# A planned instruction order made anew: planner durations set to measured occupancy, the order kept as a list of ranks

## The chip, the cores and the metric

The kernel runs on one core of a Trainium2 chip. The metric is the device time of one launch in microseconds (us): a median of 256.72 us over three runs before the change (256.70 to 256.86). The profile is that of one execution, with a span of 255.3 us.

## What is computed

Sliding-window attention with sink tokens, followed by a ResMLP block. For each of 4 batches there are 8 heads, 768 positions and head size 64:

```python
scores = scale * np.matmul(q, k.transpose(0, 1, 3, 2))
keep = (pos[None, :] < n_sink) | ((rel >= 0) & (rel < window))      # n_sink 4, window 128
a = softmax(np.where(keep, scores, -1e9))
x = heads_side_by_side(np.matmul(a, v))                              # [4, 768, 512]
a1 = alpha1 * x + beta1
u = x + lam * np.einsum('ts,bsd->btd', w_tok, a1)
a2 = alpha2 * u + beta2
out = u + lam * (np.maximum(a2 @ w_ch1, 0.0) @ w_ch2)                # w_ch1 512 x 2048, w_ch2 2048 x 512
```

Inputs and output are float32; the kernel multiplies in float16.

## The kernel before, in words

A batch is cut into six tiles of 128 tokens. Its work on TensorE falls into these groups:

- `tp`: transposes of q and k into `qkT`, in batches 0 and 1. In batches 2 and 3 DMA transposes do this, issued by SP.
- `S`, `sk`: scores of a key tile against 256 queries, and of the sink keys. ScalarE makes `E` with an exponential; VectorE or GpSimd masks it, except where a bias was added in the scores.
- `pv`: the product with v, whose row sums come with it; VectorE divides (L850, L851) and so makes `x`. GpSimd multiplies by lam times alpha1 (`tm`, L869), and VectorE or GpSimd adds the beta term (`xh`, L872).
- `tok`: the token mix, six matmuls of 512 columns for a tile (L956). VectorE adds it to `x` (L963), and ScalarE or GpSimd casts the sum to `u16` (line L356 or L358, a helper for all copies).
- `uT`: `u` transposed, in two chunks of three tiles each. In batch 0 TensorE transposes (`uTp`, L997); in the others it is a DMA transpose of each tile in SP's queue (L1015). ScalarE (L980) or VectorE (L982) then multiplies by alpha2 and adds beta2, one instruction for each of four column blocks of a chunk.
- `h`: the first MLP product, 16 feature blocks for each chunk, four matmuls of 384 columns each (L1036), and a ReLU on ScalarE or VectorE into `hT` (L1042, L1044). A chunk's `h` can start only when its four `uT` blocks are there.
- `ch` (batch 0, L1221) and `P` (batches 1 to 3, L1153): the second MLP product. In batches 1 to 3 it is one level of Strassen's scheme: seven products `P1` to `P7` of half the size, for which VectorE makes sums of `hT` (L1094 to L1097), and sums of w2 once (`w2s`, L1068).

None of this is executed in the order in which the code names it. Every group, copy and load is a task, given to `Plan.add` with a priority, the engines which could do it with a duration in ns for each, the tasks that it needs, and the buffers that it uses. `Plan.run` is a list scheduler: it repeatedly takes the task that can start first, by its own clock of every engine, with the priority deciding between equals, picks the engine that would finish it first, and adds `SEEN` ns until others see the result. It also models DMA rings (`lands`: packets, ns for each) and the shared port of VectorE and GpSimd. `Plan.emit` then issues the instructions in that order. The durations therefore never reach the chip; they decide only the order in each engine's queue, the engine of tasks with a choice, and which physical buffer each tile gets. In the first 36 us the planner also puts filler matmuls (`idle`, L349) where it expects TensorE to wait.

Before the change the priorities are those written in the code, jittered by 30 seeds one after the other (`TURNS`, through `shuffle`).

Loads on SP's queue are held back by `gates`: three tiny DMAs that read a quarter of w1 each, so that SP stands still until that quarter is there.

The functions which the change touches:

Of the kernel before, what the change touches and what calls it, by code (L numbers as in the profile page):

```python
# [10 lines left out]
FP16 = mybir.dt.float16  # L11
# [6 lines left out]
SEEN = {PE: 200, ACT: 60, DVE: 60, POOL: 70}  # L18
# [93 lines left out]
class Plan:  # L112
# [19 lines left out]
    def run(self, prio):  # L132
# [16 lines left out]
        free = {PE: 0.0, ACT: 3500.0, DVE: 3200.0, POOL: 500.0, SP: 0.0}  # L149
# [18 lines left out]
        def pick():  # L168
            best = None
            spare = {k: sorted(h for h, x in zip(homes[k], busy[k]) if not x) for k in homes}  # L170
            for r, i in open_:
# [12 lines left out]
                for e in t.engs:  # L184
                    at_e = max(free[e], at)
                    if e == POOL or (e == DVE and t.port):
                        at_e = max(at_e, port)
                    key = (at_e + FW * t.engs[e], at_e, r, at_e + t.engs[e], i, e)
                    if own is None or key < own:
                        own = key  # L190
# [55 lines left out]
    def emit(self, turns):  # L246

        prio = [t.prio for t in self.tasks]
        for seed in turns:
            prio = shuffle(prio, seed)  # L250
        for t, e, start, stop, idle in self.run(prio):
# [10 lines left out]


def shuffle(prio, seed):

    rnd = random.Random(seed)
    if seed >= 200000:
        lo = rnd.choice((12.0, 24.0, 40.0, 60.0, 100.0, 130.0, 160.0, 200.0, 230.0, 260.0, 300.0, 330.0))
        hi, wide = lo + 60.0, 10.0 ** rnd.uniform(0.3, 1.3)
    elif seed < 100000:  # L270
        lo, hi, wide = -2200.0, 8.0, 10.0 ** rnd.uniform(0.7, 2.7)
    else:
        lo = rnd.choice((0.0, 0.0, 0.0, 50.0, 100.0, 200.0))
        hi, wide = lo + 60.0, 10.0 ** rnd.uniform(0.3, 1.3)
    share = 10.0 ** rnd.uniform(-2.5, -1.0)
    return [p + rnd.gauss(0.0, wide) if lo <= p < hi and rnd.random() < share else p for p in prio]
# [3 lines left out]
def kernel(  # L280
# [128 lines left out]
    gates = sb.tile([1, 32], FP16, tag="pt_1", bufs=1, name="gates")  # L409
# [7 lines left out]
    TURNS = (13523, 134113, 50022, 128275, 136711, 187603, 125671, 100730, 14946, 163131, 178432, 158827, 183776, 137680, 153375, 26742, 367527, 307353, 376563, 212018, 255075, 397706, 218147, 375675, 393913, 224567, 207692, 352780, 243076, 346008)  # L417
# [74 lines left out]
    def load_qk(p, b, hp, t, wait=None):  # L492
# [8 lines left out]
        if b < XB:  # L501
            src = src.rearrange("h (p r) d -> p h (r d)", p=P)
            done["nat", b, hp, t] = add(
                p, {SP: 480}, lambda e: nc.sync.dma_start(bf.t, src), [wait], [bf], lands=(16, {(0, 0, 1): 85, (0, 1, 0): 140}.get((b, hp, t), 72)))
        else:
            src = src.rearrange("h s d -> (h s) d").rearrange("(x p) d -> p x d", p=P)
            done["nat", b, hp, t] = add(
                p, {SP: 700}, lambda e: nc.sync.dma_start(
                    bf.t.rearrange("p e (r d) -> p (e r) d", r=NR), src), [wait], [bf], lands=(96, 19.0))

    def load_v(p, b, r, wait=None):
        bf = vn[b, r] = Buf("vnat", None, None, f"vnat{b}_{r}")
        done["vn", b, r] = add(
            p, {SP: 550}, lambda e: nc.sync.dma_start(
                bf.t, v[b, :, r * P : (r + 1) * P, :].rearrange("h p d -> p h d")),
            [wait], [bf], lands=(64, 19.0))
# [3 lines left out]
    def load_v0(p, G, r):  # L520
# [4 lines left out]
        else:  # L525
# [7 lines left out]
            uses=[bf], lands=(32, 19.3))  # L533
# [14 lines left out]
    def load_w(p, key, src):  # L548
        bf = wst[key] = Buf("wst", None, None, f"wst_{key}")
        done["wst", key] = add(  # L550
            p, {SP: 400}, lambda e: nc.sync.dma_start(bf.t, src), [done.get(("w1", GATES[0]))], uses=[bf], lands=(16, 90))

    def load_w1(p, i):
# [4 lines left out]
            lands=(32, 96), since=W1_SINCE)  # L558

    def gate(i):  # L560

        add(-3000, {SP: 420}, lambda e: nc.sync.dma_start(
# [14 lines left out]
    ANY = {DVE: 560, ACT: 831, POOL: 829}  # L577
# [6 lines left out]
    def trans(p, b, hp, t, engs, evac, cast_p=None, wait=None):  # L584
# [43 lines left out]
        if b >= XB:  # L628
            done["qkT", b, hp, t] = add(
                p, {SP: 1240}, lambda e: nc.sync.dma_start_transpose(  # L630
                    o.t[:, 2 * hp + t, :].rearrange("p (r i) -> p r i", r=NR),
                    n16().rearrange("p r i -> p (r i)")),
                [a] + prior, [bn, o], lands=(6, 100))
# [5 lines left out]
    def sinks(p, b, Gs=(0, 1)):  # L639
# [24 lines left out]
        a = add(p, {DVE: 400 if n == 1 else 600, ACT: 440}, ksf, qk + [done.get(("sk", b - 1, 0))], [o], port=True)  # L664
        a = add(p + 0.1, {PE: 215}, mm, [a], [o, pt], mode="col")
        done["sk", b, Gs[0]] = a
        done["es", b, Gs[0]] = add(p + 0.2, {ACT: 595}, ex, [a], [pt, es[b]])

    def fill_vs(p, b, G=None):
# [13 lines left out]
        done["vs", b, G] = add(p + 0.1, {DVE: 150 + 68 * n}, ev, [a, done["vs1"]] + prior, [pt])  # L683
# [6 lines left out]
    def scores(p, b, j, Gs, bias=False):  # L690
# [51 lines left out]
        for G, hps, n, pS, eT in units:  # L742
# [7 lines left out]
            x_ = add(p + 0.1, {ACT: 170 + 2 * n * w * 0.835}, ex, [a], [pS, eT])  # L750
            if not bias:
# [11 lines left out]
                c = {DVE: 60 + 2 * n * w * 0.66}  # L763
                if b and j:
                    c[POOL] = 2 * (150 + n * w * 0.9)
# [6 lines left out]
    def scores_by_pair(p, j, bias):  # L772
# [5 lines left out]
        for hp in range(2):  # L778
# [19 lines left out]
            xs.append(add(p - 1000 + 40 * hp + 0.1, {ACT: 170 + 2 * w * 0.835}, ex, [a], [pS, eT]))  # L798
        if not bias:
# [5 lines left out]
            xs = [add(p - 999.8, {DVE: 60 + 4 * w * 0.61}, mk, xs, [eT], port=True)]  # L805
# [3 lines left out]
    def pv(p, b, r, G):  # L809
# [44 lines left out]
        a = done["x", b, r, G] = add(p + 0.1, {DVE: 640}, norm, [a], [po, rec, bx])  # L854
        prior = [done.get(("tok", b - 1, ti)) for ti in range(NR)]
        if b == 0:
            c = slice(256 * G, 256 * G + 256)

            def half(e):
# [4 lines left out]
                p + 0.3, {POOL: 730}, half, [a, done["la1"]], [bx, bh], port=True)  # L864
        elif G == 1:
# [5 lines left out]
            def plus(e):  # L871
                engine[e].tensor_add(bh.t, bt.t, lb1_b)  # L872

            a = add(p + 0.3, {POOL: 1350}, mul, [a, done["x", b, r, 0], done["la1"]], [bx, bt], port=True)
            done["xh", b, r, 1] = add(
                p + 0.4, {POOL: 1390, DVE: 690}, plus, [a, done["lb1b"]] + prior, [bh, bt], port=True)
            done["xb", b, r] = None
        if G == 1 and b == 0:
            def beta(e):
# [5 lines left out]
                (1.5 if r < 3 else 4.5) if b == 0 else p + 0.4, {DVE: 740}, beta,  # L885
# [11 lines left out]
    def cast_v0(p, G, rs):  # L897
# [3 lines left out]
            p, {POOL: 190 + 215 * n, ACT: 195 + 213 * n, DVE: 215 + 115 * n},  # L901
# [7 lines left out]
    def cast_wtok(p, ti):  # L909
# [8 lines left out]
        def cast(e):  # L918
# [8 lines left out]
        a = done["rs", ti] = add(p, {ACT: 850, DVE: 870}, cast, [done["wtn", ti]], [src, w])  # L927
        a = add(p + 0.1, {PE: 330}, tr, [a, done["iden"]], [w, pt])
        done["wtokT", ti] = add(
            p + 0.2, {DVE: 560, ACT: 810}, lambda e: copy(e, wtokT[:, :, ti * P : (ti + 1) * P], pt.t),  # L930
            [a], [pt])

    def cast_w2(p, i):
        for a in range(4 * i, 4 * i + 4):
            src = wst[f"w2_{a - a % 2}"]
            done["w2", a] = add(
                p, {DVE: 980, POOL: 1400},
# [9 lines left out]
    def tok(p, b, ti):  # L947
# [26 lines left out]
        a = done["u", b, ti] = add(p + 0.1, {DVE: 690}, ua, [a, done["xb", b, ti]], [pt, bx])  # L974
        done["u16", b, ti] = add(p + 0.2, {ACT: 620, POOL: 640}, uc, [a], [bx, bu])
# [9 lines left out]
    def uTp(p, b, chk, cp):  # L985
# [15 lines left out]
        for ci in range(2):  # L1001
            c = 2 * cp + ci
            done["uT", b, chk, c] = add(
                p + 0.1 + 0.01 * ci, {DVE: 470, ACT: 670},
# [4 lines left out]
    def uTx(p, b, ti):  # L1009

        if (b, 0) not in uT:
# [3 lines left out]
            p, {SP: 1220}, lambda e: nc.sync.dma_start_transpose(  # L1015
                bo.t[:, :, ti * P : (ti + 1) * P], bu.t),
            [done["u16", b, ti]], [bu, bo], lands=(6, 100))
# [3 lines left out]
        for c in range(NC):  # L1021
            o = (c, slice(chk * NTOK, (chk + 1) * NTOK))
            done["uT", b, chk, c] = add(
                p + 0.1 + 0.01 * c, {DVE: 380, ACT: 700},
# [3 lines left out]
    def mlp1(p, b, chk, fi):  # L1028
# [20 lines left out]
        done["h", b, chk, fi] = add(p + 0.1, {ACT: 493, DVE: 556}, relu, [a], [ph, bh])  # L1049
# [7 lines left out]
    def w2_sums(p):  # L1057

        for g in range(HF // 2):
# [5 lines left out]
            def sub(o, i0, i1, after, n_):  # L1065
# [3 lines left out]
                return add(p + 4 * g + n_, {DVE: 420, POOL: 1400}, f_, after, [bw], port=True)  # L1069
# [47 lines left out]
    def prod(p, b, what, nt):  # L1117
# [46 lines left out]
        def plus(p, bx, cols, more):  # L1164
# [3 lines left out]
            return add(p, {DVE: 400}, f_, [a, u_] + more, [pc, bx])  # L1168

        def store(p, bx, ti, cols, after):  # L1170
            n_ = (cols.stop - cols.start) // 64
            add(p, {SP: 480}, lambda e: nc.sync.dma_start(out[b, ti * P : (ti + 1) * P, cols], row(bx)[:, cols]),
# [3 lines left out]
        if what == "P1":  # L1176
            done["read", b, what, nt] = add(p + 0.1, {ACT: 390, DVE: 350}, lambda e: copy(e, bt.t, pc.t), [a], [pc, bt])
# [4 lines left out]
        elif what == "P6":  # L1182
# [3 lines left out]
            u = add(p + 0.1, {DVE: 400}, u2, [a, done["read", b, "P1", nt]], [pc, bt])  # L1186
# [4 lines left out]
            def ob(e):  # L1191
# [4 lines left out]
            done["U12", b, nt] = add(p + 0.3, {POOL: 760, DVE: 400}, ot, [u, done["u16", b, nt]], [bt, top], port=True)  # L1196
            done["U2", b, nt] = add(
                p + 0.2, {POOL: 1300, DVE: 690}, ob,
# [13 lines left out]
    def mlp2(p, b, ti, part):  # L1212
# [16 lines left out]
        if part == 3:  # L1229
# [4 lines left out]
            a = add(p + 0.1, {DVE: 690}, oa, [a, done["u16", b, ti]], [pc, bx])  # L1234
            add(p + 0.2, {SP: 480}, lambda e: nc.sync.dma_start(
# [194 lines left out]
```

The softmax here doesn't subtract the row's maximum and nothing guards it: scores larger than these inputs give would overflow.

## Time and profile before

| what | value |
|---|---|
| time | 256.72 us |
| span of the profiled execution | 255.3 us |
| TensorE (PE) busy | 247.4 us, 97% |
| VectorE (DVE) busy | 190.0 us, 74% |
| ScalarE (ACT) busy | 142.6 us, 56% |
| GpSimd (POOL) busy | 88.3 us, 35% |
| TensorE clock granted | 0.999 |
| moved by DMA | 38.8 MB, 152 GB/s over the span |

In the page, "busy" is the union of an engine's instructions; the ends of matmuls are modelled, so gaps of TensorE are better taken from starts. `A <- B` in the view of waits reads: A stood idle until B released it. The timeline merges instructions of one form and gives the start, the time from the first start to the last end, and in brackets the idle time of the engine before it with its releaser.

### The profile page before, as it was taken

How to read it: one execution, taken by the hardware profiler on the slowest of the kernel's cores; microseconds unless marked ns; L12 is line 12 of the kernel's file. 1: busy time of each engine (PE TensorE's matmuls, PEld its weight loads, DVE VectorE, ACT ScalarE, POOL GpSimd, SP SyncE). 2: the span in 40 equal slices, each digit the busy share in tenths (PEclk: the TensorE clock that was granted, in tenths of full speed). 3: DMA queues.
4: the chain of work that ended last, by engine and by line, in shares of the span. 5: the costliest groups of instructions: out<-in, count | busy, mean ns of one | idle time of the engine just before them, and what ended most of it. 6: DMA issues, size and time to landing. Idle time of an engine off the chain costs nothing.

```text
span 255.3 us, 5519 instructions
## 1 busy us (share of the span) xinstructions
PE 247.4 (97%) x2174; PEld 160.9 (63%) x2174; DVE 190.0 (74%) x402; ACT 142.6 (56%) x236; POOL 88.3 (35%) x108
## 2 busy tenths in 40 slices
PE   8999998999999999899999999999999999999994
PEld 7754645675555544456678676558668666667883
DVE  6777998696878878578889997877789764136782
ACT  2689845989848035688971225867571125775000
POOL 7409802344445330159653460735310101000000
PEclk9999999999999999999999999999999999999999
DMA  6998999999943998599778689501000156000105
GB/s 202 195 223 292 216 230 392 373 370 218 218 73 115 186 260 190 117 205 220 155 138 182 125 191 251 85 3 21 3 0 3 59 167 146 0 0 3 63 4 185
DMA packets 86130, 38.80 MB, mean 152 GB/s; under 512 B 73540, under 2 KB 80460, under 8 KB 86104
## 3 DMA queue, kind: packets, MB, share of 16 engines
q1 hardware_dynamic: 82320, 35.14, 56.5%
q0 software_dynamic: 3744, 3.28, 8.1%
q8 instruction: 17, 0.28, 0.5%
q14 instruction: 9, 0.07, 0.1%
q10 hardware_dynamic: 40, 0.03, 0.0%
HBM read 29.91 MB, written 6.29 MB: 142 GB/s over the span
## 4 chain that ended last, share of the span: by engine, by line
PE 88%; DMA 4%; DVE 3%; POOL 1%; issue 1%; ACT 1%; POOLq 0%; ACTq 0%
PE h L1036 33%; PE P L1153 21%; PE tok L956 11%; PE ch L1221 8%; PE pv L825 5%; PE S L724 4%; DMA n<-in_q_dram 4%; DVE uT L982 1%; PE S L719 1%; PE tp L614 1%; PE pv L818 1%; POOL n L497 1%; PE wT L916 1%; ACT uT L980 1%; DVE w2f L1068 1%
## 5 line engine op out<-in xcount | busy, mean ns | idle before, releaser
L1036 PE MATMUL h<-uT,w1f 128*128 128x384 f16 x512 | 91.9, 326 | 2.7 <-DVE uT L982 1.3
L1036 PEld LDWEIGHTS <-w1f 128*128 128x128 f16 x512 | 47.3, 98 | 34.5 <-issue 5.5
L1042 ACT ACTIVATE hT<-h 128x384 f16<-128x384 f32 x99 | 48.3, 492 | 26.1 <-PE h L1036 25.6
L1153 PEld LDWEIGHTS <-hT 128*128 128x128 f16 x408 | 39.8, 98 | 6.7
L746 ACT ACTIVATE E<-S 128x1024 f16<-128x1024 f32 (+1 forms) x39 | 37.9, 1001 | 7.5 <-PE S L724 3.7
L869 POOL TENSOR_TENSOR tm<-x,la_b 128x512 f32<-128x512 f32 x18 | 26.2, 1454 | 26.3 <-DVE xh L872 19.1
L956 PE MATMUL tok<-xh,wtokT 128*128 128x512 f16 x144 | 33.4, 379 | 0.0
L356 ACT CAST u<-x 128x512 f16<-128x512 f32 x19 | 11.7, 618 | 31.2 <-DVE x L963 31.1
L1153 PE MATMUL P<-w2f,hT 128*128 128x256 f16 x216 | 25.9, 273 | 0.0
L1166 DVE TENSOR_TENSOR x<-x,P 128x256 f32<-128x256 f32 x45 | 18.3, 418 | 8.2 <-PE P L1153 7.9
L1044 DVE TENSOR_SCALAR hT<-h 128x384 f16<-128x384 f32 x29 | 15.8, 553 | 10.9 <-PE h L1036 10.5
L956 PEld LDWEIGHTS <-wtokT 128*128 128x128 f16 x144 | 14.0, 98 | 14.6
L1221 PE MATMUL ch<-w2f,hT 128*128 128x512 f16 x96 | 23.0, 379 | 0.0
L1153 PE MATMUL P<-w2s,hT 128*128 128x256 f16 x192 | 22.8, 273 | 0.0
L851 DVE TENSOR_TENSOR x<-pv,rec 128x256 f32<-128x256 f32 x48 | 20.4, 424 | 1.7
L358 POOL CAST vfs<-vnat 128x512 f16<-128x512 f32 x18 | 15.0, 840 | 16.2 <-DMA vnat<-in_v_dram 16.0
L963 DVE TENSOR_TENSOR x<-x,tok 128x512 f32<-128x512 f32 x24 | 16.2, 684 | 5.7 <-PE tok L956 5.7
L356 ACT CAST n<-nat 128x768 f16<-128x768 f32 x16 | 13.2, 829 | 10.8 <-DMA nat<-in_q_dram 8.8
L825 PEld LDWEIGHTS <-E 128*128 128x128 f16 x328 | 15.2, 97 | 6.0 <-issue 1.6
L825 PE MATMUL pv<-vfs,E 128*128 128x65 f16 x328 | 17.9, 194 | 0.0
L358 POOL CAST u<-x 128x512 f16<-128x512 f32 x5 | 3.1, 621 | 34.8 <-DVE x L963 21.1
L1221 PEld LDWEIGHTS <-hT 128*128 128x128 f16 x96 | 8.6, 98 | 9.1 <-issue 0.2
(131 smaller groups left out, 327.4 us busy)
## 6 DMA issues: line engine op xcount, KB each, us to landing
out_dram<-x SPq DMA_DIRECT2D x21, 256.0 KB, 2.8
nat<-in_q_dram SPq DMA_DIRECT2D x13, 384.0 KB, 5.3
nat<-in_k_dram SPq DMA_DIRECT2D x13, 384.0 KB, 5.7
vnat<-in_v_dram SPq DMA_DIRECT2D x18, 256.0 KB, 5.2
wst_w<-in_moe_w_ch_dram SPq DMA_DIRECT2D x8, 512.0 KB, 7.4
wtn<-in_moe_w_tok_dram SPq DMA_DIRECT2D x6, 384.0 KB, 4.7
w1f<-in_moe_w_ch_dram POOLq DMA_DIRECT2D x4, 512.0 KB, 11.1
v<-in_v_dram SPq DMA_DIRECT2D x12, 128.0 KB, 6.4
```

The costliest lines, as they stand in the source:

```text
L356: nc.scalar.copy(o, i)
L358: engine[e].tensor_copy(o, i)
L746: nc.scalar.activation(eT.t, pS.t[:, :, 0 : n * w].rearrange("p e (i w) -> p e i w", i=n), AF.Exp, scale=scale)
L825: nc.tensor.matmul(po.t[:, hl, :], eT.t[:, e_, off + i, c : c + P], vf[j][:, h, :], start=(r < 2 and n == 0), stop=(n == len(parts) - 1 an ...
L851: nc.vector.tensor_mul(bx.t[:, 4 * G : 4 * G + 4, :], po.t[:, :, 0:D], rec.t.to_broadcast([P, 4, D]))
L869: engine[e].tensor_mul(bt.t, bx.t.rearrange("p h d -> p (h d)"), la1_b)
L956: nc.tensor.matmul(pt.t, wtokT[:, si, ti * P : (ti + 1) * P], hs[si].t, start=(si == 0), stop=(si == NR - 1))
L1036: nc.tensor.matmul(ph.t, w1f[:, c, fi * P : (fi + 1) * P], bu.t[:, c, chk * NTOK : (chk + 1) * NTOK], start=(c == 0), stop=(c == NC - 1))
L1042: nc.scalar.activation(bh.t[:, fi, :], ph.t, AF.Relu)
L1153: nc.tensor.matmul(pc.t, hh[:, nt * P : (nt + 1) * P], w(fi), start=(first and n_ == 0), stop=(n_ == HF - 1), skip_group_check=True)
L1166: nc.vector.tensor_add(row(bx)[:, cols], row(bx)[:, cols], pc.t)
L1221: nc.tensor.matmul(pc.t, bh.t[:, fi, nt * P : (nt + 1) * P], w2f[:, fi, :], start=(fi == 0), stop=(fi == NF - 1))
```

## The change

It is for a plan whose clock is nearer to that of the chip, and an order searched for on it. Four things change:

1. The durations of nearly all tasks on ScalarE, VectorE, GpSimd and SP are set to the measured occupancy of the engine (how long until it can take the next), which is shorter than the instruction's latency; in exchange `SEEN`, the time until a reader may start, grows from 60 to 150 ns on ScalarE and VectorE. DMA packets get new times too, and GpSimd and SP start later in the plan (500 to 1600 ns, 0 to 800 ns).
2. The order is no longer code priorities jittered by seeds, but a list of 1143 ranks, one for each task (`ORDER`).
3. A string of digits (`PINS`) can fix the engine of a task: 0 leaves the choice, n takes the n-th of its engines.
4. The tile `gates` gets a place of its own instead of sharing one with a later buffer, since two of the gates now stand late in SP's queue.

```diff
-SEEN = {PE: 200, ACT: 60, DVE: 60, POOL: 70}
+SEEN = {PE: 200, ACT: 150, DVE: 150, POOL: 70}
...
-    def run(self, prio):
+    def run(self, prio, pin=None):
...
-        free = {PE: 0.0, ACT: 3500.0, DVE: 3200.0, POOL: 500.0, SP: 0.0}
+        free = {PE: 0.0, ACT: 3500.0, DVE: 3200.0, POOL: 1600.0, SP: 800.0}
...
-                for e in t.engs:
+                one = pin[i] if pin and pin[i] <= len(t.engs) else 0
+                for n, e in enumerate(t.engs):
+                    if one and n + 1 != one:
+                        continue
...
-    def emit(self, turns):
-        prio = [t.prio for t in self.tasks]
-        for seed in turns:
-            prio = shuffle(prio, seed)
-        for t, e, start, stop, idle in self.run(prio):
+    def emit(self, prio, pin):
+        for t, e, start, stop, idle in self.run(prio, pin):
...
-    gates = sb.tile([1, 32], FP16, tag="pt_1", bufs=1, name="gates")
+    gates = const.tile([1, 32], FP16, name="gates")
...
-    TURNS = (13523, 134113, 50022, 128275, 136711, 187603, 125671, 100730, 14946, 163131, 178432, 158827, 183776, 137680, 153375, 26742, 367527, 307353, 376563, 212018, 255075, 397706, 218147, 375675, 393913, 224567, 207692, 352780, 243076, 346008)
+    ORDER = (
+        66, 71, 1075, 86, 311, 53, 58, 60, 63, 54, 64, 61, 65, 67, 81, 95, 68, 69, 72, 62, 77, 74,
...
-                p, {SP: 480}, lambda e: nc.sync.dma_start(bf.t, src), [wait], [bf], lands=(16, {(0, 0, 1): 85, (0, 1, 0): 140}.get((b, hp, t), 72)))
+                p, {SP: 480}, lambda e: nc.sync.dma_start(bf.t, src), [wait], [bf], lands=(16, {(0, 0, 1): 85, (0, 1, 0): 140}.get((b, hp, t), 68)))
...
-        add(-3000, {SP: 420}, lambda e: nc.sync.dma_start(
+        add(-3000, {SP: 790}, lambda e: nc.sync.dma_start(
...
-            x_ = add(p + 0.1, {ACT: 170 + 2 * n * w * 0.835}, ex, [a], [pS, eT])
+            x_ = add(p + 0.1, {ACT: 50 + 2 * n * w * 0.85}, ex, [a], [pS, eT])
...
-                c = {DVE: 60 + 2 * n * w * 0.66}
+                c = {DVE: 70 + 2 * n * w * 0.53}
...
-            a = add(p + 0.3, {POOL: 1350}, mul, [a, done["x", b, r, 0], done["la1"]], [bx, bt], port=True)
+            a = add(p + 0.3, {POOL: 1250}, mul, [a, done["x", b, r, 0], done["la1"]], [bx, bt], port=True)
...
-                p, {DVE: 980, POOL: 1400},
+                p, {DVE: 612, POOL: 1240},
...
-        a = done["u", b, ti] = add(p + 0.1, {DVE: 690}, ua, [a, done["xb", b, ti]], [pt, bx])
-        done["u16", b, ti] = add(p + 0.2, {ACT: 620, POOL: 640}, uc, [a], [bx, bu])
+        a = done["u", b, ti] = add(p + 0.1, {DVE: 610}, ua, [a, done["xb", b, ti]], [pt, bx])
+        done["u16", b, ti] = add(p + 0.2, {ACT: 530, POOL: 575}, uc, [a], [bx, bu])
...
-        done["h", b, chk, fi] = add(p + 0.1, {ACT: 493, DVE: 556}, relu, [a], [ph, bh])
+        done["h", b, chk, fi] = add(p + 0.1, {ACT: 395, DVE: 480}, relu, [a], [ph, bh])
...
-    plan.emit(TURNS)
+    plan.emit(ORDER, [int(c) for c in PINS])
```

The instructions themselves, their number on TensorE (2174 matmuls, 106 of them filler) and the data moved stay as they were. In the new order, the groups of TensorE around the places of which the prediction speaks are these (`b` the batch; a group of `h`, four matmuls; of `tok`, six; of `ch`, four; of `P`, eight):

| place | before | after |
|---|---|---|
| batch 0, `tok` to `h` | six `tok`, `uTp` x2, `h` | five `tok`, `uTp` x2, `tok` of tile 5, `h` |
| batch 1, `tok` to `h` | `tok` 1, 0, 2, `ch`, `tok` 3, 4, 5, `h` | `tok` 0, 2, 1, `ch`, `tok` 5, `ch`, `tok` 3, `ch`, `tok` 4, `h` |
| batch 2, late `tok` to chunk 1 of `h` | `tok` 4, then 2 `h`, 2 `S`, 2 `pv`, 6 `P` | `tok` 3, then 2 `h`, 2 `S`, 4 `pv`, 4 `P` |
| batch 3, `tok` to `h` | `tok` 5, then `h` of chunk 0 | `tok` 3, 4, 2, 5, 2 `P`, `tok` 0, `P`, `tok` 1, 3 `P`, `h` of chunk 1 |

## The prediction

> **What bounds the kernel now.** First the page: its busy shares, its slices, the chain that ended last.
>
> ```profile
> PE 247.4 (97%) x2174; PEld 160.9 (63%) x2174; DVE 190.0 (74%) x402; ACT 142.6 (56%) x236; POOL 88.3 (35%) x108
> ...
> PE   8999998999999999899999999999999999999994
> ...
> PEclk9999999999999999999999999999999999999999
> ...
> PE 88%; DMA 4%; DVE 3%; POOL 1%; issue 1%; ACT 1%; POOLq 0%; ACTq 0%
> ```
>
> TensorE is nearly always occupied, at full clock, and is 88% of the chain. No instruction disappears in this change, so a new order can only take away TensorE's waiting. How much there is, the view of TensorE's waits says (us in total, times, longest):
>
> ```profile
> PE h L1036 <- DVE uT L982: 1.3, 2, 1.1
> PE idle L349 <- DVE warm L375: 1.1, 1, 1.1
> PE h L1036 <- ACT uT L980: 0.9, 2, 0.5
> PE tp L611 <- DMA n<-in_q_dram: 0.5, 1, 0.5
> PE h L1036 <- DVE x L1166: 0.4, 1, 0.4
> ```
>
> After the start, all of it stands before an `h` matmul: the first MLP product waits for `uT`, the transposed and scaled token-mix result. The timeline of TensorE shows the two large seams, batch 0 first, then batch 1 (start us, us):
>
> ```profile
> 38.47 0.83 PE L997 MATMUL uTp<-iden,u 128*128 128x128 f16 x12
> 39.78 0.32 PE L1036 MATMUL h<-uT,w1f 128*128 128x384 f16 x1 [0.47 <-ACT uT L980]
> 40.29 0.71 PE L1036 MATMUL h<-uT,w1f 128*128 128x384 f16 x2 [0.19 <-DVE uT L982]
> 41.38 0.48 PE L1036 MATMUL h<-uT,w1f 128*128 128x384 f16 x2 [0.38 <-ACT uT L980]
> ```
>
> ```profile
> 96.85 1.03 PE L1221 MATMUL ch<-w2f,hT 128*128 128x512 f16 x4
> 97.71 4.05 PE L956 MATMUL tok<-xh,wtokT 128*128 128x512 f16 x18
> 102.83 1.35 PE L1036 MATMUL h<-uT,w1f 128*128 128x384 f16 x5 [1.07 <-DVE uT L982]
> ```
>
> Ends of matmuls are modelled, so I go by starts. Batch 0: the last transposes start at 39.08 and need 0.06, three `h` matmuls need 3 x 0.163; up to 41.38 that leaves 1.75 us lost. Batch 1: the last `tok` matmul starts at 101.38 and streams 0.216, so 1.23 lost, and another 0.26 inside the first `h` group: 1.5. A third one (a `P` matmul at 179.56, `h` at 180.20) is 0.53. Together **3.8 us**. From 182 to the last matmul there is no gap over 0.1: 128 `h` matmuls take 20.80 us in the chain (162.5 ns each), 168 `P` matmuls 18.35 (109 ns).
>
> The start (0 to 31 us) is of another kind: 106 filler matmuls (L349) stand where TensorE has nothing to do while q and k land, and ScalarE is busy 22.5 of 31 us.
>
> **What the Trainium skill says.** (1) Perfetto Trace Analysis, "Optimizing Scalar/DVE Operations": the profiled latency contains a write-acknowledgement half that overlaps the next instruction, so it is longer than the time for which the engine is taken. The trace agrees: four adds `x<-x,tok` in a row took 2.58 us from 34.79, a spacing of 0.63, with a mean of 684 ns for one. The new planner entry is 610, the old one 690. (2) Same page, "Identifying the Most-Contended Engine": matmul busy share is no measure of headroom. Agreed: TensorE is called 97% busy, yet its starts show the 3.8 us above. (3) TensorE: Matmul & The Clock Gate, "Back-to-back issue gap": N/2.4 + 2.5 ns when warm; 162.5 ns for N = 384 agrees exactly. The 131 ns that it gives for N = 512 with weight loads this trace doesn't show: a `tok` group of six takes 1.29 us, 215 ns each. (4) SBUF, "SBUF: two separate sides": VectorE and GpSimd hold their shared port pair exclusively. In this trace GpSimd's `tm` multiply (L869) takes 1.27 us in some places, 1.65 in another, mean 1454 ns; the new entry for it is 1250, so GpSimd may run later than planned.
>
> **The change, part by part.**
>
> *Durations, SEEN.* They cost nothing on the chip. A ReLU on ScalarE was 493 + 60 = 553 ns from start to a reader, and becomes 395 + 150 = 545: latency kept, occupancy 98 less. The plan may now put more between two dependent pieces, but leaves less slack on a full queue. All that counts on the chip is the new order.
>
> *Work per engine* (counting both orders): TensorE the same 2174 matmuls, 106 fillers in both. Four qkT copies go from ScalarE to VectorE (one in batch 0, three in batch 1), three wtokT copies the other way; GpSimd gives three masks (1.2 us each) to VectorE and takes four w2f products and three u16 casts. No engine's total moves by more than about 3 us, and only TensorE's waits matter.
>
> *Start.* Up to the first `tok`, the new TensorE order has one score group (0.75) ahead of the last two transposes instead of behind them, one small product (0.28) the other way, and four wtokT transposes in the stretch in both. But ScalarE gets 3.2 us of wtokT copies instead of 1.6 there, and one more 0.4 us `ks` pair. Summing its new list from its first copy (7.8 us) to the last wtokT copy gives 23.9 us against 23.5 before, which had 1.0 idle: it ends at 31.7 to 32.7 against 32.6. The last q load is issued about 1.6 us later on GpSimd, behind the mask building, but its ring has a backlog (it took 9.4 us before). I take 0, with -0.8 to +0.8.
>
> *Batch 0 seam.* Before, all six `tok` groups came first, then the transposes, and TensorE waited. Now `tok` of tile 5 (1.29 us) stands between the transposes and the first `h`. The four scalings need about 1.7 us (three VectorE at 0.43 start to start, one ScalarE at 0.67, plus handover), so 0.4 stays: **-1.35**, bounds -1.75 to -0.8. The new `h` order wants all four quarters of w1 within seven groups (4.6 us); before they landed 10.2 to 12.0 us after issues at 21.0 to 27.6, so by 39.6, as `h` starts.
>
> *Batch 1 seam.* First chunk: its third `tok` group ended at 96.85, `h` ran freely from 103.41, a chain of 6.56 us (add, cast, DMA transposes in SP's queue, four scalings, of which VectorE had three behind a 0.69 add of another tile). What TensorE had meanwhile was one `ch` part (0.86) and three `tok` groups: 4.74. Now it has three `ch` parts and three `tok` groups, 6.45; the scalings are two and two, with no such add ahead of them. Chain about 6.0: **-1.5**, bounds -1.5 to -0.5.
>
> *Batch 2.* First chunk: two `tok` groups and seven product halves (0.87), 8.7 us of filler, enough for either chain. Second chunk (the 0.53 before): 8.2 us of filler stood after the late `tok` group, now 6.8. VectorE's queue from that group's add to the last scaling, at the mean spacings (masks 0.68, norms 0.6, ReLU 0.55, `xh` 0.68, copies and scalings 0.36), sums to 7.3 us: a wait of 0.6 to 1.5. Taken: **+0.4** over the 0.53.
>
> *Batch 3.* Last-mixed chunk: 6 x 0.87 + 2 x 1.29 = 7.8 us of filler, no wait. Other chunk: 5 x 0.87 + 4 x 0.65 = 6.95 against 6.0 to 6.6: **+0.1**. The end has the same three P3 halves and stores: 0.
>
> Other moved groups (ReLUs between 41 and 250 us, w2f products) lie beside `h`, `ch` and `P` streams which had no gap; I cost them at nothing, hidden by those. Sum: 0 - 1.35 - 1.5 + 0.4 + 0.1 = -2.35: 256.72 - 2.35 = **254.4 us**.
>
> **The rivals.**
> - *The start gets shorter as well*, for start times of GpSimd (1.6 us, seen 1.83) and SP (0.8, seen 0.81) are now right: another -1.8, 252.5. Against it: the same 106 fillers are planned, and ScalarE's list is no shorter.
> - *The gain is eaten* by waits of 0.1 to 0.3 us between scores, masks and pv, as queues are planned tighter: +2.3, about 256.7. For: GpSimd's entries are below its means. Against: the old order, from wrong durations, has almost none.
> - *Slower*: VectorE takes seven w2f products (0.64 each, 4.5 us) before batch 0's second-chunk scalings. If w2 lands 3 us later than the 41 us of before, for the batch 1 loads are no longer held back by the second and third gate, `h` stops for that long, and batch 2's second chunk takes its 1.5: 256.72 - 2.85 + 3 + 1 + 0.3 = about 258.2. For: DMA is 91% busy from 41 to 93 us.
>
> **How the numbers follow.** Forecast 0.64, start shorter 0.12, eaten 0.08, slower 0.16. Faster by over 0.2%: 0.64 + 0.12 + a little of "eaten", 0.77; within 0.2%, 0.06; slower 0.17. The range: low 252.0 (all seams closed, start -0.8, and the first rival mostly), high 257.2 (eaten, and the milder part of slower).
>
> **What would show it.** Right: TensorE's wait of `h` for uT falls from 2.2 us to under 1; after the transposes of batch 0 comes a `tok` group; the first `h` of batch 1 carries no wait on VectorE; the late chunk of batch 2 keeps 0.5 to 1.5. Wrong: a start stage that moves by over 1 us either way, new waits of `pv` or `P` on VectorE or GpSimd, or `h` waiting for w1 or for scalings behind w2f at 45 to 50 us.

## The result, and the profile after

The changed kernel takes **258.61 us** (median of 4 runs, 257.6 to 258.88), the kernel before 256.79 beside it: a ratio of 1.0062, interval 1.0033 to 1.0091. It is slower, by about 1.6 us as the ratio has it; 254.4 had been forecast. Run again later, unedited, it took 258.81 us (1.0082, 1.0059 to 1.0104; median of five runs, a sixth at 262.59 was an execution in the core's slower state, which the ratios here leave out).

The page of the changed kernel, busy shares and the chain that ended last:

```profile
PE 247.6 (96%) x2174; PEld 160.8 (63%) x2174; DVE 188.0 (73%) x395; ACT 142.7 (56%) x237; POOL 95.1 (37%) x111
...
PE 75%; DVE 12%; DMA 8%; ACT 1%; issue 1%; POOL 1%; SPq 0%; ACTq 0%; DVEq 0%
```

TensorE's work is unchanged, VectorE is even 2 us less busy, and yet VectorE's share of the chain rose from 3% to 12%: TensorE now waits for things that stand in VectorE's queue. What it waits for (us in total, times, longest). Lines of this kernel are 64 higher than before, so L1100 is `h`, L1046 and L1044 are the scalings (of `uT` by alpha2 and beta2), L915 is a norm (the division after `pv`) and L1230 the P add; the helper for copies is L340 and L342:

```profile
PE wT L980 <- ACT wt L985: 1.1, 2, 0.9
PE idle L333 <- DVE warm L359: 1.1, 1, 1.1
PE h L1100 <- DVE uT L1046: 0.9, 1, 0.9
PE h L1100 <- DVE x L1230: 0.6, 1, 0.6
PE h L1100 <- ACT uT L1044: 0.6, 1, 0.6
PE h L1100 <- DVE x L915: 0.5, 1, 0.5
PE pv L889 <- DVE x L915: 0.2, 1, 0.2
PE tp L678 <- DVE qkT L342: 0.2, 1, 0.2
```

The first two lines belong to the start. Of the rest, the same view before had `h` waiting for scalings and an add, and nothing for norms or `qkT`. The wait of batch 0's first `h` (1.75 us, taken from starts) is down to 0.24. The wait at batch 1's seam (the passage from `tok` to `h`) is still there, and there are new ones.

To see where the time came from, I charged every matmul with the usual start-to-start spacing of its kind (the lower quartile over both traces); what remains of the elapsed time is lost time. Its difference to the kernel before, in us (the last column is the mended kernel of experiment 7):

| up to | changed | changed, second trace | mended |
|---|---|---|---|
| 30 us (start) | 0.00 | -0.01 | -0.01 |
| 45 us (batch 0 seam) | -1.09 | -1.51 | -1.50 |
| 95 us | +0.61 | +1.69 | -0.23 |
| 150 us (batch 1 seam, batch 2 attention) | +0.57 | +1.64 | -1.59 |
| 200 us | +1.05 | +2.12 | -2.05 |
| last matmul | +1.08 | +2.14 | -2.03 |

The batch 0 gain is there. It is lost, with more, before 95 us; the batch 1 seam gives almost nothing; 150 to 200 us costs another half.

**Four places in the trace of the changed kernel.** Below, a wait at a place is the start-to-start time beyond the usual spacing; the page's own figure, from modelled ends, is 0.1 to 0.2 smaller. The first is 48 us, where the second chunk's `h` should start (0.71):

```profile
44.78 2.49 DVE L1002 TENSOR_TENSOR w2f<-wst_w,lam_b 128x512 f16<-128x512 f32 x4
...
47.18 0.86 DVE L1046 TENSOR_SCALAR uT<-uTp,ab 128x384 f16<-128x384 f16 x2
47.69 1.23 ACT L1044 ACTIVATE uT<-uTp,ab 128x384 f16<-128x384 f16 x2 [0.71 <-DVE uT L1046]
...
48.98 0.48 PE L1100 MATMUL h<-uT,w1f 128*128 128x384 f16 x2 [0.55 <-ACT uT L1044]
```

Seven w2f products (w2 times lam) and a sum, begun at 42.55 after 1.32 us of waiting for w2, stand in VectorE's queue before its two scalings; ScalarE's two start only when VectorE's first is done. In the kernel before, VectorE had seven such products at this time too, but all four of these scalings ran on ScalarE:

```profile
41.13 1.46 DVE L938 TENSOR_TENSOR w2f<-wst_w,lam_b 128x512 f16<-128x512 f32 x1
...
42.98 3.69 DVE L938 TENSOR_TENSOR w2f<-wst_w,lam_b 128x512 f16<-128x512 f32 x6
```

```profile
44.08 0.67 ACT L980 ACTIVATE uT<-uTp,ab 128x384 f16<-128x384 f16 x1
...
45.06 1.23 ACT L980 ACTIVATE uT<-uTp,ab 128x384 f16<-128x384 f16 x2
...
46.54 0.69 ACT L980 ACTIVATE uT<-uTp,ab 128x384 f16<-128x384 f16 x1
```

The second is 102 us, batch 1's seam (1.04):

```profile
101.11 0.69 DVE L1296 TENSOR_TENSOR x<-x,ch 128x512 f32<-128x512 f32 x1 [0.17 <-PE ch L1285]
101.63 1.15 POOL L1132 TENSOR_TENSOR w2f<-w2f 128x512 f16<-128x512 f16 x1
101.71 1.48 DVE L1046 TENSOR_SCALAR uT<-uT,ab 128x384 f16<-128x384 f16 x2
...
103.24 0.48 PE L1100 MATMUL h<-uT,w1f 128*128 128x384 f16 x2 [0.88 <-DVE uT L1046]
```

The data was there at 100.89 (ScalarE began its half then). VectorE first waited for a `ch` product and added it to another tile; then GpSimd started a w2 difference, and the first of the two scalings took 1.18 us, the second 0.37. The planner does not foresee this: it keeps those of VectorE's tasks that carry `port=True` apart from GpSimd's, but the scalings carry no such mark. The third place is 133 us (0.64): the last `pv` matmul of its group started at about 131.2, but the norm that frees its PSUM tile (the buffer that TensorE writes to) stands behind a mask that took 1.77 us beside GpSimd's `tm`:

```profile
131.33 1.77 DVE L825 TENSOR_TENSOR E_None<-E_None,maskn 128x1024 f16<-128x1024 f16 x1
...
133.23 0.42 DVE L915 TENSOR_TENSOR x<-pv,rec 128x256 f32<-128x256 f32 x1
...
133.71 0.50 PE L1100 MATMUL h<-uT,w1f 128*128 128x384 f16 x2 [0.48 <-DVE x L915]
```

The fourth is 176.6 us (0.75, with 0.15 just before and 0.13 after it), the wait that the forecast did expect: a mask, `xh` and a copy stand before batch 2's scalings. Here too GpSimd works beside them: `xh` took 1.12 us beside a mask on GpSimd, and the two scalings 1.61 us beside `tm`, where another `xh` took 0.68 and two scalings 0.66 (run 3). The view names the P add behind the two as what came last:

```profile
175.37 1.61 DVE L1046 TENSOR_SCALAR uT<-uT,ab 128x384 f16<-128x384 f16 x2
...
177.36 4.84 PE L1100 MATMUL h<-uT,w1f 128*128 128x384 f16 x28 [0.59 <-DVE x L1230]
```

**Theory 1**: the loss is VectorE's queue. Its work was placed by a plan that prices each task as undisturbed, and on the chip other work stands before what TensorE waits for. **Rivals**: w2 and w1 land later (DMA); the port that VectorE shares with GpSimd; TensorE's own new order.

### The profile page after: what moved, and what is told of

Read it like the earlier page. It is cut to its first block, busy times and chain, and to the rows that moved or that the text cites. A ratio compares the mean times of both kernels' runs of the same rounds, so it can differ in the third digit from the quotient of the medians.

```text
span 256.7 us, 5493 instructions
## 1 busy us (share of the span) xinstructions
PE 247.6 (96%) x2174; PEld 160.8 (63%) x2174; DVE 188.0 (73%) x395; ACT 142.7 (56%) x237; POOL 95.1 (37%) x111
## 4 chain that ended last, share of the span: by engine, by line
PE 75%; DVE 12%; DMA 8%; ACT 1%; issue 1%; POOL 1%; SPq 0%; ACTq 0%; DVEq 0%
PE h L1100 28%; PE P L1217 19%; PE tok L1020 9%; PE ch L1285 7%; DMA w1f<-in_moe_w_ch_dram 5%; DVE E L825 3%; PE pv L889 3%; PE S L788 3%; DMA wst_w<-in_moe_w_ch_dram 2%; PE idle L333 2%; DVE x L915 2%; DVE w2f L1002 1%; DVE uT L1046 1%; PE tp L675 1%; PE tp L678 1%
## 5 line engine op out<-in xcount | busy, mean ns | idle before, releaser
L1100 PE MATMUL h<-uT,w1f 128*128 128x384 f16 x512 | 89.1, 326 | 2.6 <-DVE uT L1046 0.9
L1100 PEld LDWEIGHTS <-w1f 128*128 128x128 f16 x512 | 48.4, 98 | 35.0 <-issue 5.0
L1106 ACT ACTIVATE hT<-h 128x384 f16<-128x384 f32 x98 | 47.7, 493 | 28.0 <-PE h L1100 22.1
L1108 DVE TENSOR_SCALAR hT<-h 128x384 f16<-128x384 f32 x30 | 16.6, 555 | 24.7 <-PE h L1100 23.0
L1217 PE MATMUL P<-w2f,hT 128*128 128x256 f16 x216 | 26.7, 273 | 0.1
L340 ACT CAST n<-nat 128x768 f16<-128x768 f32 x18 | 14.8, 831 | 20.1 <-DMA nat<-in_k_dram 17.4
L342 POOL CAST vfs<-vnat 128x512 f16<-128x512 f32 x18 | 12.9, 715 | 32.3 <-DMA vnat<-in_v_dram 30.4
L340 ACT CAST u<-x 128x512 f16<-128x512 f32 x16 | 9.9, 618 | 22.9 <-DVE x L1027 22.8
L915 DVE TENSOR_TENSOR x<-pv,rec 128x256 f32<-128x256 f32 x48 | 20.4, 424 | 1.7
L1230 DVE TENSOR_TENSOR x<-x,P 128x256 f32<-128x256 f32 x45 | 18.2, 416 | 4.5 <-PE P L1217 4.0
L825 DVE TENSOR_TENSOR E<-E,maskn 128x1024 f16<-128x1024 f16 x20 | 16.4, 833 | 0.0
```

The source lines that it names most:

```text
L340: nc.scalar.copy(o, i)
L825: nc.vector.tensor_mul(ev, ev, m.to_broadcast(list(ev.shape)))
L915: nc.vector.tensor_mul(bx.t[:, 4 * G : 4 * G + 4, :], po.t[:, :, 0:D], rec.t.to_broadcast([P, 4, D]))
L1100: nc.tensor.matmul(ph.t, w1f[:, c, fi * P : (fi + 1) * P], bu.t[:, c, chk * NTOK : (chk + 1) * NTOK], start=(c == 0), stop=(c == NC - 1))
L1106: nc.scalar.activation(bh.t[:, fi, :], ph.t, AF.Relu)
L1217: nc.tensor.matmul(pc.t, hh[:, nt * P : (nt + 1) * P], w(fi), start=(first and n_ == 0), stop=(n_ == HF - 1), skip_group_check=True)
```

## The experiments

All edits but those of runs 2 and 12 move single tasks later in the order in which instructions are issued, by a few lines in `Plan.emit`; everything else stays. (i, j) puts task i right behind task j. Lines of these kernels are 7 higher (8 in run 2). Ratios are to the kernel before in the same session.

```diff
+MOVES = ((181, 278), (200, 181), (199, 200), (202, 199))
+HOMES = {}
...
-        for t, e, start, stop, idle in self.run(prio, pin):
+        steps = self.run(prio, pin)
+        for i, j in MOVES:
+            s = steps.pop(next(n for n, s in enumerate(steps) if s[0].i == i))
+            steps.insert(1 + next(n for n, s in enumerate(steps) if s[0].i == j), s)
+        for t, e, start, stop, idle in steps:
+            e = HOMES.get(t.i, e)
```

**1. Four products behind the scalings** (the diff above: 181, 200, 199 and 202 are w2f products, 278 a ReLU).

> The changed kernel, with four of VectorE's seven early w2f products of batch 0 (w2 tiles 0, 13, 12, 15) put behind the two second-chunk scalings and two ReLUs that stood after them; nothing else. Theory 1 (the new order loses its gain in VectorE's queue: work queued on a planned landing time stands before what TensorE waits for): the 0.71 us that h waits at 48.1 goes (under 0.15), TensorE is 0.7 us ahead at 60 us, and the kernel takes about 257.9 us, ratio to the kernel before about 1.004. Rival 2 (DMA: w1 and w2 landing later): h or ch waits for the landing instead, no gain, 258.6. Rival 3 (the gain is eaten later, since the waits at 57, 71 and 102 us grow): the wait at 48 goes but the time stays within 0.2 of 258.6.

Measured: 257.6 us, ratio 1.0037 (1.0025 to 1.0049). VectorE idled 2.75 us before the scalings, and the wait at 48 fell from 0.71 to 0.36, not under 0.15. Theory 1 holds for half of that wait. Neither `h` nor `ch` waited for a landing.

**2. The same order, without waiting for w2.**

```diff
-                lambda e, a=a, src=src: engine[e].tensor_mul(w2f[:, a, :], src.t[:, a % 2, :], lam_b),
+                lambda e, a=a, src=src: engine[e].tensor_mul(
+                    w2f[:, a, :], lam_b if a in (0, 1, 6, 7, 12, 13, 15) else src.t[:, a % 2, :], lam_b),
```

> The changed kernel in its own order, but the seven early w2f products on VectorE multiply lam by lam, a tile long resident, so they don't wait for w2 (the product of these seven tiles with w2 is left out; duration and place in the queue are the same). If the wait at 48.1 needs the late landing (VectorE stood idle 1.32 us for w2 at 41 to 42.5), the scalings come 1.3 us earlier and the 0.71 us wait falls under 0.1: about 257.9 us. If the seven products alone fill VectorE too long, the scalings still come too late and a wait of 0.3 or more stays: 258.3 us.

Measured: 259.38 us, ratio 1.0097 (1.0084 to 1.011). No gain: to take away the wait for w2 is not enough. TensorE's pace was another in this run's trace (a span of 287.3 us), so its waits are not compared. VectorE's queue can be read: the products began as soon as VectorE was free, and from the first of them to the first scaling it took 8.0 us (43.13 to 51.14) instead of 4.63; beside six GpSimd instructions, four of the seven products took 1.09 to 1.75 us each. Runs 3, 6, 9 and 11, in which w2 landed at different times by itself, show the same two sides.

**3. and 4. The batch 1 seam, two causes apart.** Run 3 takes the w2 difference (task 354) from GpSimd; run 4 puts the add of `ch` (333) and its store (334) behind the scaling 468.

```diff
+MOVES = ((354, 350),)
+HOMES = {354: DVE}
```

```diff
+MOVES = ((333, 468), (334, 333))
+HOMES = {}
```

> The changed kernel with one w2f difference (1.15 us on GpSimd, which ran at 101.63 beside the first-chunk scalings of batch 1) moved to VectorE, behind three others of its kind that follow the scalings. If GpSimd's use of the shared port is what made the first scaling 1.18 instead of 0.37 us, two scalings take 0.67 us, h starts 0.8 us earlier (the wait of 0.88 falls to about 0.1 to 0.3) and the time is about 257.8. If the add of another tile ahead of the scalings (theory 1, queue) is the whole cause, nothing changes: the wait stays 0.8 or more, 258.6.

> The changed kernel with the add of x0_4 and ch0_4 on VectorE (0.69 us, waiting 0.17 for ch) put behind the two first-chunk scalings of batch 1 that followed it, and its store behind it. Theory 1 (queue): the scalings start at 100.9 to 101.1 instead of 101.7, before GpSimd starts its difference at 101.6, so h starts 1.0 us earlier, wait under 0.2: 257.6 us. Port rival: the second scaling falls into GpSimd's difference and ends at 102.8 or later as before: no gain, 258.6.

Run 3: 257.78 us, ratio 1.0040 (1.0025 to 1.0054). VectorE's scalings, and `h` after them:

```profile
101.94 0.66 DVE L1053 TENSOR_SCALAR uT<-uT,ab 128x384 f16<-128x384 f16 x2
...
102.65 0.65 PE L1107 MATMUL h<-uT,w1f 128*128 128x384 f16 x3
```

Two scalings take 0.66 instead of 1.48 us, the wait is 0.23 instead of 1.04. Run 4: 257.25 us, ratio 1.0019 (1.0003 to 1.0035):

```profile
100.88 0.96 DVE L1053 TENSOR_SCALAR uT<-uT,ab 128x384 f16<-128x384 f16 x2
...
102.23 0.98 PE L1107 MATMUL h<-uT,w1f 128*128 128x384 f16 x5
```

The scalings now run before GpSimd's difference (at 101.69), and the wait is 0.02. Both causes are shown, the queue and GpSimd's instruction, and either edit nearly closes the seam: the add ahead shifted the scalings by 0.8 us into GpSimd's instruction, which held them for another 0.8.

**5. Crossed scalings.** As run 1, and with (248, 242): ScalarE starts on one PSUM tile, VectorE on the other.

> The changed kernel with the four w2f products behind the second-chunk scalings of batch 0 (as in the run before) and, besides, VectorE and ScalarE starting on different PSUM tiles of uTp: ScalarE takes its half of tile 1 first, VectorE its half of tile 0 first. In the first run 0.36 us of the wait at 48 was left, and ScalarE began its first scaling 0.1 us after VectorE's first ended, although its data was there: if the two engines are held one behind the other on the same PSUM tile, crossing them makes ScalarE start 0.4 us earlier, the 0.36 falls under 0.1 and the time is about 257.3. If ScalarE simply had no data earlier (rival), the 0.36 stays: 257.6 to 257.9.

Measured: 257.36 us, ratio 1.0023 (1.0011 to 1.0036). ScalarE's first scaling starts at 46.47, with the last transposes, instead of 47.14, and 0.14 of the wait at 48 is left. ScalarE had been held by VectorE's reading of the same tile, as expected. The Trainium skill (PSUM — Partial Sum Buffer, "PSUM bank collisions raise a hardware error") says that two engines must not access the same partitions of one bank at once, and that the compiler orders them. Who sets the order here no run shows; the order itself is there: in the changed kernel ScalarE's first scaling starts at 47.69, and VectorE's first ends at 47.66. Another wait grew in this trace, 0.96 at 117 us, where it is 0.29 in the changed kernel.

**6. The attention stretches alone.** 706 is the mask of the third place (133 us), 710 the norm; 933 is `xh`, 824 a P add, 943 GpSimd's next `tm`, 748 the last scaling on VectorE.

```diff
+MOVES = ((706, 710), (933, 748), (824, 748), (943, 933))
+HOMES = {}
```

> The changed kernel with only VectorE's order in two attention stretches changed: in batch 2 (132 us) the last mask multiplication goes behind the norm that frees h's PSUM tile; in batch 3 (174 us) the xh add (and GpSimd's next tm multiplication, which reuses its tile) and one P add go behind the three second-chunk scalings. Theory 1 (queue): the waits of 0.64 at 133 and 0.75 at 176.6 fall to under 0.15 and 0.3, the kernel takes about 257.5 us (ratio 1.003). Rival (the masks and xh that now come later stop pv and tok by as much): no gain, 258.4 to 258.6.

Measured: 258.73 us, ratio 1.0092 (1.0059 to 1.0125): no gain in time, against theory 1. In the trace the two edited places did what was expected:

```profile
133.04 0.42 DVE L922 TENSOR_TENSOR x<-pv,rec 128x256 f32<-128x256 f32 x1
...
133.38 1.22 DVE L832 TENSOR_TENSOR E_None<-E_None,maskn 128x1024 f16<-128x1024 f16 x1
...
134.56 0.33 PE L1107 MATMUL h<-uT,w1f 128*128 128x384 f16 x1
```

The norm is now ahead of the mask and `h` starts without a wait (0.64 before); at 177 us 0.62 is left of 0.88. But in this execution the wait at 48 was 1.43 instead of 0.71, and `pv` waited 1.35 at 119 us instead of 0.29, for two masks that took 2.75 us beside GpSimd. So in time this run shows no gain, and none of the others has these edits alone; run 7 has them with the rest.

**7. All the edits together**: the moves of runs 1, 4, 5 and 6.

> The changed kernel with all these moves in VectorE's queue together: products behind the batch 0 scalings, crossed scalings, the add of x0_4 behind the batch 1 scalings, batch 2's mask behind the norm, batch 3's xh behind the scalings. TensorE's instructions are in the changed kernel's own order. If the whole loss of the change is VectorE's queue (theory 1), the four parts add: 258.6 - 0.7 - 1.0 - 0.6 - 0.6 = 255.7 us, faster than the kernel before by 0.4% (ratio about 0.996). If part of it is given back downstream (rival): 256.5 to 257, not distinguishable from the kernel before. If TensorE's new order itself were the cause (rival), it would stay above 257.5.

Measured: **255.24 us**, ratio **0.9944** (0.9929 to 0.9959): 3.0 to 3.5 us faster than the changed kernel, by the ratios of its two sessions, and faster than the kernel before. TensorE's matmuls are issued in the changed kernel's order; only VectorE's tasks, one of GpSimd's and one store were moved. It is near theory 1's 255.7, and TensorE's new order as the cause of the loss is refuted. What stands ahead in VectorE's queue and what GpSimd does beside it are not told apart by this run, since its moves change both; runs 3 and 4 do that for the seam at 102 us, where both count. The whole view of TensorE's waits:

```profile
PE wT L987 <- ACT wt L992: 1.1, 1, 1.1
PE idle L340 <- DVE warm L366: 1.1, 1, 1.1
PE h L1107 <- DVE hT L1115: 0.5, 1, 0.5
PE P L1224 <- DVE x L1237: 0.2, 1, 0.2
PE tp L685 <- DVE qkT L349: 0.2, 1, 0.2
```

In this view no `h` waits for a scaling or a norm any more; one waits for a ReLU (0.60 us at 63 us by starts). Its runs also lie close (12 of 13 within 254.96 to 255.82, one at 257.53), where those of the changed kernel lie between 257.60 and 259.75.

**8. One part alone, on the kernel before**: its last `tok` group of batch 0 behind the transposes, its add and cast behind the scalings.

```diff
+MOVES = ((226, 223), (227, 224), (228, 227))
```

> The kernel before with one part of the change alone: in batch 0 the last tok group (1.29 us, tile 3) goes behind the two uTp transposes, its add on VectorE and its cast on GpSimd behind the first-chunk scalings. By the prediction's step for batch 0 TensorE loses 1.75 us at this seam in the kernel before and 0.4 after this: about 255.4 us, ratio 0.995. If the gain is given back at the next seam (second chunk's transposes wait for tile 3's cast), 256.0 to 256.7.

Measured: 256.24 us, ratio 0.9983 (0.9973 to 0.9993). A gain of about 0.5 us, not 1.3: of the 1.75 us of waiting, 1.03 stays, for ScalarE's scalings, of which this kernel has two on the path where the changed one has one. So the moved `tok` group alone takes 0.72 us off this wait, about half of what the changed kernel takes off (1.51). That the other half comes from the scalings' new engines is argued from the traces; no run has these alone.

**9. GpSimd's product away, the seven still ahead.** 201 is that product, 363 a cast, 355 the w2 sum.

```diff
+MOVES = ((201, 363), (355, 201))
```

> The changed kernel with GpSimd's one early w2f product (w2 tile 14, 1.3 to 1.8 us, which stood beside VectorE's seven) put behind GpSimd's first two k and q casts of batch 1, and the w2 sum that reads it behind it; VectorE's seven products stay ahead of the second-chunk scalings. In the runs so far the wait at 48 us grew as w2 landed earlier: first product at 42.55, 41.2, 40.7 us, wait 0.71 or 0.37, 1.01, 1.43. If GpSimd's product stretches VectorE's products by holding the shared port (port theory), the seven take 0.6 each in every run, VectorE is free by 46.2 and the wait at 48 falls to the 0.36 that the crossed scalings removed, when w2 lands by 41.5: about 257.9 us. If the seven products are too many whatever GpSimd does (queue alone), 0.7 or more stays: 258.6.

Measured: 258.41 us, ratio 1.0053 (1.0035 to 1.0071). **11** is the changed kernel again:

> The changed kernel once more, unedited, for its spread and a second trace: 258.6 us, with waits before h at 48 (0.4 to 1.4 by how w2's landing and GpSimd's product meet), 102 (1.0), 133 (0.6) and 176 us (0.75). If the waits are of the order and not of one run, the last three return within 0.1 us; the first and those at 71 and 118 us, which need VectorE and GpSimd to meet, differ.

258.81 us, as above. Its waits at 103, 134 and 178 us return (1.04, 0.64, 0.75); the one at 48 is 2.05. VectorE, GpSimd and TensorE there:

```profile
43.37 4.81 DVE L1002 TENSOR_TENSOR w2f<-wst_w,lam_b 128x512 f16<-128x512 f32 x4
...
43.57 1.61 POOL L1002 TENSOR_TENSOR w2f<-wst_w,lam_b 128x512 f16<-128x512 f32 x1 [1.59 <-DMA wst_w<-in_moe_w_ch_dram]
...
46.60 2.27 POOL L342 CAST n<-nat 128x768 f16<-128x768 f32 x2 [0.19 <-DMA nat<-in_q_dram]
...
48.11 0.85 DVE L1046 TENSOR_SCALAR uT<-uTp,ab 128x384 f16<-128x384 f16 x2
...
49.89 0.32 PE L1100 MATMUL h<-uT,w1f 128*128 128x384 f16 x1 [1.89 <-ACT uT L1044]
```

Four products took 4.81 us here, 2.49 in the first trace. Six traces with this queue (us):

| run | first product (w2 is there) | from it to the first scaling | first scaling | wait of `h` |
|---|---|---|---|---|
| 9 (GpSimd idle until 49.1) | 43.04 | 4.64 | 47.68 | 1.02 |
| changed, first | 42.55 | 4.63 | 47.18 | 0.71 |
| 4 | 42.55 | 4.63 | 47.18 | 0.37 |
| 3 | 41.20 | 5.87 | 47.07 | 1.01 |
| 6 | 40.72 | 6.75 | 47.47 | 1.43 |
| changed, second | 40.73 | 7.38 | 48.11 | 2.05 |

(In run 4 TensorE itself was 0.34 later.) When w2 lands late, VectorE waits for it; when it lands early, GpSimd's product and the k and q casts, released by the same stream of transfers, overlap VectorE's products and stretch them. The scalings come between 47.1 and 48.1 either way. The latest landing (run 9, with GpSimd idle) and the earliest (the second trace, with products stretched) both gave over 1 us of waiting: a late landing is one of two ways to the wait, and it isn't needed. What the six have in common are the seven products ahead. In runs 1, 5, 7 and 10, with only three products ahead, VectorE was ready by the time of the transposes whether the first product ran at 40.73 or 41.73. In run 9 the stretching is gone, but w2 landed latest of all, so it doesn't measure the wait without GpSimd and with an early landing. An estimate: run 9's 4.64 us from the earliest start, 40.73, would end at 45.4, before the transposes (45.87 to 46.7 in run 7).

**10. One more wait of the mended kernel**: the moves of run 7, and two products at 60 us behind two ReLUs.

```diff
+         (183, 300), (195, 274)
```

> The mended kernel of the run before (255.24 us) with two w2f products of VectorE at 60 us put behind the two ReLUs that stood after them; in its trace h waited 0.60 us at 62.35 for such a ReLU, while three products took 3.6 us beside GpSimd's three. Queue theory: this wait goes, 254.7 us, ratio 0.992. Rival: the products then delay the masks at 64 us and pv waits instead: 255.2 us.

Measured: 254.96 us, ratio 0.9932 (0.9913 to 0.9951); not to be told from run 7. The 0.60 at 63 us went, and `pv` waited 0.82 at 68 us for a mask instead of under 0.1: both theories came true in part.

**12. The durations alone**, with the old priorities and seeds.

```diff
-    plan.emit(ORDER, [int(c) for c in PINS])
+    plan.emit(TURNS)
```

> The durations of the change alone: the planner has the new durations, start times and SEEN, and sets the order from the old priorities with their 30 shuffles, not from the new list of ranks and pins. Those shuffles were made for other durations, so they now mean nothing. If the new durations by themselves bring work of VectorE ahead of what TensorE waits for (theory 1 put down to the durations), the waits before h at 40 to 50 and 100 us are there too and it takes 258 us or more; if they make a plan that is nearer to the chip (rival), it is no slower than the kernel before, 256 to 257; if the ranks carry what the change gains at batch 0's seam, that gain (1.1 us at 45 us) is missing here.

Measured: 262.21 us, ratio 1.0223 (1.0196 to 1.0249). The waits before `h` are there at 44 (0.36) and 104 us (1.23 and 0.56), TensorE has lost 0.26 us more than in the kernel before by 50 us where the changed kernel had lost 0.38 less, and the largest wait, 2.23 at 200 us, is a `P` waiting for a VectorE add behind four sums of `hT` (3.5 us). So the durations by themselves do not bring the gain at batch 0's seam. How many of the waits come from the durations and how many from seeds that fit no more, this run doesn't separate.

## Why the prediction was wrong

- **Start, 0**: 0.00 at 30 us. Right.
- **Batch 0 seam, -1.35**: -1.1 and -1.5 in the two traces; the first has a wait of 0.40 at 32.5 us, ahead of the seam, that the second lacks. Right in size, but run 8 shows that the moved `tok` group alone brings only about half of it (the forecast's sum had the scalings' new engines in it as well).
- **"Other moved groups ... I cost them at nothing, hidden by those"**: this is the step that failed. From 45 to 95 us the changed kernel lost 1.70 us against the kernel before, and 3.20 in its second trace. Named waits are 0.71 before the second chunk's `h`, 0.34 at 57 us behind `qkT` copies and 0.41 at 71 us behind five masks in a row; in the second trace 2.05, 0.34 and, at 65 us for a ReLU, 0.59. At 133 us comes 0.64 behind a mask. The groups lay beside streams which had had no gap, but that was the old order's doing. In batch 0 the second chunk's scalings were all on ScalarE, while VectorE worked off seven products; the new order gave two of them to VectorE behind such products, and put the transposes 2.8 us later (from 46.29 instead of 43.49), with two `h` groups (1.3 us) between them and the chunk's first `h`. The forecast had counted the seven products ahead of the scalings, but only in a rival.
- **Batch 1 seam, -1.5**: measured 1.49 before, 1.04 after, so -0.45. This step failed too, by 1.05 us. "With no such add ahead of them" was false: `x0_4` plus `ch` stands before VectorE's two scalings, and moved them beside GpSimd's difference (one of the four tasks that the forecast saw go to GpSimd as w2f products, and cost at nothing). Run 4 without it leaves 0.02, which is the -1.5. From 95 to 150 us, the 0.64 included, the changed kernel gained 0.04, the mended one 1.36.
- **Batch 2, second chunk, +0.4**: 1.03 instead of 0.53, +0.5. Right in size, in part by luck: the forecast summed VectorE's queue at mean spacings (`xh` 0.68, a scaling 0.36), and in the trace `xh` took 1.12 and one scaling 1.33 beside GpSimd.
- **Batch 3, +0.1**: after 182 us the view of waits shows no wait of TensorE before an `h` or a `P`; by starts, 0.20 and 0.15 us follow two score groups. Right.
- **End, 0**: the profiled span adds 0.26 us after the last matmul in the first trace and 0.08 in the second. Right; the first is that run's.

The rival that came nearest in time, "slower" with 258.2, had the right place (products before the scalings), and in the first trace its reason too, in a smaller size: the first product came at 42.55, 1.4 us later than the 41.13 of before. In the second trace w2 was there by 40.73 and the wait was larger, for the products were stretched, which the rival did not have. The "eaten" rival had the other part, waits between masks, norms and the next product. Both had been given little weight because the old trace had almost no such waits; that was read as a property of the work, and was one of the old order. The warning was in that trace: its one w2f product beside a GpSimd product took 1.46 us where the six after it took 0.62 each (the lines are above), and the forecast used 0.64 for all.

Run 7 shows how much of the forecast gain the TensorE order can give: with the moved groups mended it takes 255.24 us, 0.56% below the kernel before where 0.9% had been forecast. It also takes away batch 2's waits, with which the forecast had reckoned, so more was due by the forecast's own terms. What is missing lies between 45 and 95 us, where the mended kernel still loses 1.27 us: 0.60 at 63 us for a ReLU behind three products, 0.34 at 57 us behind `qkT` copies, and smaller waits.

What stays open: how large the wait at 48 us would be, measured, with GpSimd silent and w2 early; whether the new durations would be better than the old ones under ranks found with them on the chip; and what the pins and the new place of `gates` do by themselves, which no run separates.

## What to carry to other kernels

When a new order keeps the bottleneck engine's work and moves that of the others, walk the queues of the others for each point where the bottleneck waits, also where it doesn't wait yet: on which engine the instruction that releases it now stands, what stands ahead of it there, and what may hold that up. One late or stretched instruction in front delayed what stood behind it in its queue (at 102 us by 0.8 us), though VectorE was busy for only 73% of the span. A planner fed with undisturbed durations packs such queues tightly; leave what the bottleneck waits for ahead of work that has time.

## What the runs showed of the hardware

- An f16 scaling from SBUF to SBUF (128x384) takes 0.37 us on VectorE alone; beside a GpSimd subtraction of 1.15 us it took 1.18 and ended 0.1 us after it. The Trainium skill (SBUF — State Buffer, "SBUF: two separate sides") calls the port an exclusive lock for the whole instruction; the trace agrees. The f16 scalings out of PSUM in batch 0, 0.86 us for two beside GpSimd's product of 1.73, were not stretched (0.85 in the second trace beside a cast, and 0.85 in run 9 with GpSimd idle).
- A chain of four products, 2.49 us in the first trace, took 4.81 us when GpSimd worked beside it: 2.3 us lost beside four GpSimd instructions of 1.61, 0.83 and (two) 2.27 us.
